# Loading V by head group in turn with the last quarters of w_out, in a fused attention and MLP kernel

## The chip, the cores and the metric

The kernel runs on one core of a Trainium2 chip. The metric is the device time of one execution in microseconds (us). The profile's own span is a little shorter than that time; both are given below.

## The reference

Attention over 8 batches, 12 heads, 448 tokens and a head dimension of 64, and then a two-layer MLP on its output (3584 tokens, model width 768, inner width 2048):

```python
scores = scale * np.matmul(q, k.transpose(0, 1, 3, 2))
scores = scores - np.max(scores, axis=-1, keepdims=True)
attn = np.exp(scores)
attn = attn / (np.sum(attn, axis=-1, keepdims=True) + 1e-09)
attn_out = np.matmul(attn, v)
...
x = attn_out.transpose(0, 2, 1, 3).reshape(B * S, H * D)
h = x @ w_in
g = h * (1.0 / (1.0 + np.exp(-h)))
return g @ w_out
```

All inputs and the output are float32 in memory; the kernel converts them to float16 as it loads them.

## The kernel before, in words

The twelve heads of a batch are taken in three head groups of four. A unit is one head group of one batch; the first batch is cut into five smaller units (`BEGIN`), so that work can start before all of it is there. For each unit the kernel loads K and Q (`load_k` into `rk`, `load_q` into `rq`), transposes them on VectorE (`turn_k` into `KT`, `turn_q`), multiplies them on TensorE into `s` (`scores`), takes the exponential on ScalarE into `E`, sums it over keys (`attend_sums`, the `a` that reads `T` and `half`, or for the first units the `a` that reads `ones`), and multiplies it with V (`attend`, the `a` that reads `V`). VectorE normalises the result into `xT`.

A batch that is through attention goes through the MLP: `ffn1` makes `h` from `w_in_t` and `xT`, ScalarE takes a tanh, VectorE's `gate` makes `G`, and products with `w_out_t` follow. The first two token tiles (`plain`, tiles `o`) use `w_out_t` as it is, in pieces of four of its sixteen row blocks, so a piece needs one quarter of `w_out`. The later ones (`product`, tiles `p`) work on pairs of token tiles with sums and differences of weights and gates, which takes fewer products; the sums of `w_out` (`combine_w`, tiles `D`) need all four quarters. The last two batches do the same with `w_in` (tiles `f`).

A product can stand on the whole array or in strips of 32 columns (`strips` in `times`): the strips are four matmuls for one, which run side by side, and are chosen where the work before was in strips as well (the mode "cols"). Scores are in the mode "rows". While TensorE has nothing else to do in the first stretch, it multiplies zeros (`run_zeros`, tile `z`, line 1602).

The order of all instructions is worked out ahead, in Python, while the kernel is built. `Order` holds a clock, a queue for each engine and estimated durations; at each step the loop at the end of the kernel takes the next work whose inputs are ready by these estimates, and the instructions are then written out in that order, each engine's for itself. On the chip each engine goes through its list in order and waits where a tile isn't there.

The loads are not reordered by it. POOL issues them in the order in which the `plan_` calls stand: `plan_k`, `plan_q`, `plan_v`, `plan_w_in` and `plan_w_out` append to `od.pool`. Their landing times are estimated in `Order.step`: a load takes slot after slot of one transfer queue (`dma_free`), starts at the earliest `DMA_START` after its issue, and is there `DMA_TAIL` after its transfer. At most `LOADS` = 8 of them may be under way, and in the built kernel each load waits for the eighth before it to land. K, Q and V also wait for a free buffer (three for `rk`, four for `rq`, two batches of V).

A V load is four transfers of 32 partitions each (`load_v`). The first batch's V is loaded for all twelve heads at once; from the second batch on it is loaded by head group. `w_out` comes in quarters of 768 KB (as float16).

Two estimates steer TensorE's order beside these: `LATE` shifts the time at which a V product of the first batch counts as ready against the landing of its V, and a weight's products count as ready once all loads in `ld_win` or `ld_wout` that they need have landed.

Of the kernel before, what the change touches and what calls it, by code (L numbers as in the profile page):

```python
# [18 lines left out]
PE_OUT = 0.20  # L19
HOP = 0.10  # L20
OVERLAP = {"ACT": 0.09, "DVE": 0.07}
LOADS, DMA_SLOW = 8, 1.45
DMA_ROW = 0.006
DMA_RATE = 13570.0
DMA_START = 1.2
DMA_TAIL = 1.5


def mm(n):
# [7 lines left out]
def rank(op):  # L37
    return (op.bias > -9) + (op.bias > 35)
# [65 lines left out]
class Order:  # L104
# [21 lines left out]
    def start(self, op):  # L126
        self.emit(op.emit)
        self.free[op.eng] = self.now + op.busy - OVERLAP.get(op.eng, 0.0)
        self.busy[op.eng] += op.busy
# [23 lines left out]
    def step(self):  # L153

        soon = []
        for eng in ("ACT", "DVE"):
            if self.free[eng] > self.now:
                soon.append(self.free[eng])
                continue
            best, urgent = None, None  # L160
            for op in self.wait[eng]:
                at = op.ready()
                if at is None:
                    continue
                if at > self.now:
                    soon.append(at)
                    if op.bias <= -10 and (urgent is None or at < urgent):
                        urgent = at
                elif best is None or (rank(op), at + op.bias) < best[0]:
                    best = ((rank(op), at + op.bias), op)  # L170
            if best and best[1].bias >= 0 and eng == "DVE" and urgent is not None:
                if urgent < self.now + self.shy * best[1].busy:
                    continue
            if best:
                self.wait[eng].remove(best[1])
                self.start(best[1])
                soon.append(self.free[eng])
        if self.free["POOL"] > self.now:
            soon.append(self.free["POOL"])
        elif self.pool:  # L180
            op, took, ring, gate = self.pool[0]
            at = 0.0
            if ring is not None:
                at = ring.when(1)
            if at is not None and len(self.sent) >= LOADS:
                at = max(at, self.sent[-LOADS].done + HOP)
            if at is not None and gate is not None:
                g = gate()
                at = None if g is None else max(at, g)
            if at is not None and at <= self.now:  # L190
                self.pool.pop(0)
                if ring is not None:
                    ring.take()
                self.start(op)
                self.sent.append(op)
                took += DMA_SLOW if len(self.sent) == 3 else 0.0
                self.dma_free = max(self.dma_free, self.now + DMA_START) + took
                op.done = self.dma_free + DMA_TAIL
                soon.append(self.free["POOL"])
            elif at is not None:  # L200
                soon.append(at)
        return soon
# [3 lines left out]
def kernel(  # L206
# [13 lines left out]
    DFF = moe_w_in.shape[1]  # L220
    HG = 4
    NG = NH // HG
# [8 lines left out]
    NFF = DFF // 128  # L231
# [6 lines left out]
    NPL = 4  # L238
    EAGER = 1
    HALVES = 0  # L240
    NEAR, LATE = 0.15, -0.9
    COLD, FIRST = 8.5, 47
    SHY = 0.5
    AWAIT = 0.0
# [5 lines left out]
    NB0 = len(BEGIN)  # L250
# [52 lines left out]
    def load_q(n):  # L303
        b, hg, g0, g1 = units[n]
        t = sb.tile([128, (g1 - g0) * D], FP16, name=f"rq_{n}", tag="rq", bufs=NRQ)
        nc.gpsimd.dma_start(out=t, in_=group_of(q, b, hg)[:, D * g0 : D * g1])  # L306
        rawq[n] = t

    def form(b, hg):
        n = NG * b + hg  # L310
        if n in LONES:
            return "lone"
        return ("low", "high")[(n - sum(x < n for x in LONES)) % 2]


    def load_v(b, hg0, hg1, x):
        if b not in VT:
            VT[b] = sb.tile([128, NH, NCH, D], FP16, name=f"V_{b}", tag="V", bufs=2)
        hs = slice(HG * hg0, HG * hg1)
        kind = form(b, hg0)  # L320
        if x == 0 and kind != "lone":
            lo = 64 if kind == "low" else 0
            nc.gpsimd.memset(VT[b][lo : lo + 64, hs, NCH - 1, :], 0.0)
        first, count = X_TOK[kind][x]
        nc.gpsimd.dma_start(  # L325
            out=VT[b][32 * x : 32 * (x + 1), hs, 0:count, :],
            in_=v[b, hs].rearrange("h (i g) d -> i h g d", g=TPP)[
                :, :, first : first + count, :
            ],
        )  # L330


    def load_w_in(c, f0, f1):
        nc.gpsimd.dma_start(
            out=w_in_t[:, 2 * c : 2 * c + 2, f0:f1],
            in_=moe_w_in[256 * c : 256 * (c + 1), f0:f1].rearrange(
                "(p j) f -> p j f", j=2
            ),
        )

    def load_w_out(f0, f1):
        nc.gpsimd.dma_start(
            out=w_out_t[:, f0:f1],
            in_=moe_w_out[128 * f0 : 128 * f1].rearrange("(f p) m -> p f m", p=128),
        )
# [106 lines left out]
    def add_e(n, step):  # L452
        if step == 0:
            T[n] = sb.tile([128, HG, S], FP16, name=f"T_{n}", tag="T", bufs=NT_)
        nc.vector.tensor_tensor(  # L455
            out=T[n],
            in0=T[n] if step else E[(n, 0)],
            in1=E[(n, step + 1)],
            op=ALU.add,
        )  # L460
# [55 lines left out]
    def inverse(ns, step, i=0):  # L516
        g0, g1 = units[ns[0]][2:]
        shape = [128, g1 - g0, 32]
        if step == 0:
            sT_t[ns[0]] = sb.tile(shape, FP32, name=f"sT_{ns[0]}", tag="sT", bufs=1)  # L520
            nc.vector.transpose(
                out=sT_t[ns[0]],
                in_=acc[(ns[0], 0)][:, 0 : 32 * (g1 - g0)].rearrange("p (g i) -> p g i", i=32),
            )
        elif step == 1:
            inv_t[ns[0]] = sb.tile(
                shape[:2] + [len(ns)], FP32, name=f"inv_{ns[0]}", tag="inv", bufs=2
            )
            nc.vector.reciprocal(
                out=inv_t[ns[0]], in_=sT_t[ns[0]][:, :, 0 : 32 : 32 // len(ns)]  # L530
            )
        else:
            n = ns[i]
            rdn_t[n] = sb.tile(shape, FP32, name=f"rdn_{n}", tag="rdn", bufs=2)
            nc.vector.transpose(
                out=rdn_t[n], in_=inv_t[ns[0]][:, :, i : i + 1].to_broadcast(shape)
            )
# [353 lines left out]
    def plan_k(b, hg):  # L891
        ld_k[(b, hg)] = od.load(128, 2 * D * TPP, lambda: load_k(b, hg), rk_ring)

    def plan_q(n):
        g0, g1 = units[n][2:]
        ld_q[n] = od.load(128, 2 * D * (g1 - g0), lambda: load_q(n), rq_ring)

    def plan_v(b, hg0, hg1):
        made = []
        for x in range(4):  # L900
            ring = v_ring if (x == 0 and hg0 == 0) else None
            heads, toks = HG * (hg1 - hg0), X_TOK[form(b, hg0)][x][1]
            made.append(
                od.load(32 * heads, 2 * D * toks, lambda x=x: load_v(b, hg0, hg1, x), ring)
            )
        for hg in range(hg0, hg1):
            ld_v[(b, hg)] = made

    def plan_w_in(f0, f1):
        made = [  # L910
            od.load(256, 2 * (f1 - f0), lambda c=c: load_w_in(c, f0, f1))
            for c in range(NG)
        ]
        for f in range(f0 // 128, f1 // 128):
            ld_win[f] = made

    def plan_w_out(f0, f1):
        wout_rows.append(f0)
        ld_wout.append(od.load(128 * (f1 - f0), 2 * DM, lambda: load_w_out(f0, f1)))
# [7 lines left out]
    plan_v(0, 0, NG)  # L927
    plan_q(3)
    plan_q(4)
    plan_w_in(0, DFF // 4)  # L930
    plan_w_in(DFF // 4, DFF // 2)
    plan_k(1, 0)
    plan_q(NB0)
    plan_w_in(DFF // 2, DFF)
    plan_k(1, 1)
    plan_q(NB0 + 1)
    plan_w_out(0, NFF // 4)
    plan_w_out(NFF // 4, NFF // 2)
    plan_k(1, 2)
    plan_q(NB0 + 2)  # L940
    for hg in range(NG):
        plan_v(1, hg, hg + 1)
    plan_w_out(NFF // 2, 3 * NFF // 4)
    plan_w_out(3 * NFF // 4, NFF)
    for n in range(NB0 + NG, NU):
        b, hg = units[n][:2]
        plan_k(b, hg)
# [750 lines left out]
```

## Time and profile before

| | |
|---|---|
| Median of 3 runs | 390.31 us (390.11 to 392.94) |
| The profiled execution | 390.07 us, span 388.3 us |
| TensorE (PE) | 380.2 us busy |
| VectorE (DVE) | 270.0 us |
| ScalarE (ACT) | 250.2 us |
| GpSimd (POOL) | 90.8 us, mostly issuing loads |

In the rows of the profile, PE is TensorE's matmuls, PEld its weight loads, and L577 is line 577 of the kernel before. A row of the order of time has the start in us, the duration in us, engine, line and operation, what is written and read, shapes and type, and the number of instructions that are merged. A bracket at its end is the time for which the engine stood idle before it, and what ended that. A row of waits has the engine and line, what it waited for, the total in us, how often, and the longest. "DMA to landing" is the time from a load's issue to the landing of its last byte, as the least, the median and the greatest of the group. GB/s counts bytes written. A row of the stages has the stretch in us, then for PE, PEld, DVE, ACT and POOL the busy time and the number of instructions, the granted TensorE clock, the share of the DMA engines and GB/s.

### The profile page before, as it was taken

How to read it: one execution, taken by the hardware profiler on the slowest of the kernel's cores; microseconds unless marked ns; L12 is line 12 of the kernel's file. 1: busy time of each engine (PE TensorE's matmuls, PEld its weight loads, DVE VectorE, ACT ScalarE, POOL GpSimd, SP SyncE). 2: the span in 40 equal slices, each digit the busy share in tenths (PEclk: the TensorE clock that was granted, in tenths of full speed). 3: DMA queues.
4: the chain of work that ended last, by engine and by line, in shares of the span. 5: the costliest groups of instructions: out<-in, count | busy, mean ns of one | idle time of the engine just before them, and what ended most of it. 6: DMA issues, size and time to landing. Idle time of an engine off the chain costs nothing.

```text
span 388.3 us, 10882 instructions
## 1 busy us (share of the span) xinstructions
PE 380.2 (98%) x4504; PEld 199.4 (51%) x4504; DVE 270.0 (70%) x544; ACT 250.2 (64%) x383; POOL 90.8 (23%) x175
## 2 busy tenths in 40 slices
PE   7999989999999999999999999999999999999995
PEld 3467755444554444455445554554445655556663
DVE  2565757989977696967798758567869964447441
ACT  4898864697775979676874667466783238882220
POOL 6742365507006331600643024000000000000000
PEclk9999999999999999999999999999999999999999
DMA  7999999908236763924956139002000130001333
GB/s 111 200 210 209 169 157 216 195 12 111 52 78 102 139 81 40 137 72 92 136 80 84 42 76 161 11 2 61 24 1 2 43 97 26 0 2 40 92 95 101
DMA packets 36002, 34.54 MB, mean 89 GB/s; under 512 B 11376, under 2 KB 35184, under 8 KB 35952
## 3 DMA queue, kind: packets, MB, share of 16 engines
q0 software_dynamic: 25456, 22.82, 39.9%
q1 hardware_dynamic: 10080, 10.53, 10.0%
q8 instruction: 35, 0.57, 0.7%
q10 hardware_dynamic: 416, 0.49, 0.4%
q14 instruction: 15, 0.12, 0.1%
HBM read 45.61 MB, written 11.01 MB: 146 GB/s over the span
## 4 chain that ended last, share of the span: by engine, by line
PE 88%; DMA 8%; POOL 1%; DVE 1%; issue 0%; ACT 0%; DVEq 0%; POOLq 0%
PE p L577 31%; PE h L577 24%; PE s L407 10%; PE a L470 9%; PE f L577 8%; DMA rq<-in_q_dram 6%; PE o L577 2%; DMA w_out_t<-in_moe_w_out_dram 2%; PE a L486 2%; PE z L1602 1%; PE z L470 1%; POOL V L325 1%; PE z L577 0%; DVE rq L378 0%; POOL rk L300 0%
## 5 line engine op out<-in xcount | busy, mean ns | idle before, releaser
L444 ACT ACTIVATE E<-s 128x896 f16<-128x896 f32 (+1 forms) x172 | 148.0, 916 | 32.3 <-PE s L407 31.7
L577 PE MATMUL h<-xT,w_in_t 128*32 128x448 f16 (+2 forms) x1308 | 116.0, 340 | 0.0
L577 PEld LDWEIGHTS <-w_in_t 128*32 128x32 f16 (+1 forms) x1392 | 71.7, 97 | 56.2 <-issue 11.3
L609 ACT ACTIVATE th<-h 128x448 f16<-128x448 f32 x95 | 51.8, 546 | 35.2 <-PE h L577 31.6
L577 PEld LDWEIGHTS <-G 128*128 128x128 f16 (+1 forms) x652 | 43.5, 97 | 33.7 <-issue 5.5
L868 ACT COPY ost<-p 128x384 f32<-128x384 f32 x52 | 24.9, 480 | 53.2 <-PE p L577 50.2
L653 DVE SCALAR_TENSOR_TENSOR G<-th,h 128x448 f16<-128x448 f16 (+1 forms) x80 | 44.0, 557 | 14.9 <-ACT th L609 14.5
L325 POOL DMA_DIRECT2D V<-in_v_dram x88 | 48.3, 560 | 16.5 <-DMA w_out_t<-in_moe_w_out_dram 6.1
L577 PE MATMUL p<-w_out_t,G 128*128 128x384 f16 (+1 forms) x376 | 49.6, 326 | 0.0
L407 PE MATMUL s<-rq,KT 32*128 32x448 f16 (+4 forms) x736 | 45.4, 345 | 1.5 <-DVE rq L378 1.4
L577 PEld LDWEIGHTS <-S 128*128 128x128 f16 (+1 forms) x408 | 29.9, 98 | 23.0 <-issue 3.1
L470 PE MATMUL a<-E,V 128*32 128x448 f16 (+3 forms) x800 | 40.3, 342 | 0.0
L306 POOL DMA_DIRECT2D rq<-in_q_dram x26 | 14.5, 559 | 100.0 <-PE s L407 90.5
L577 PE MATMUL p<-D,S 128*128 128x384 f16 (+1 forms) x256 | 37.2, 326 | 0.0
L874 DVE TENSOR_TENSOR ost<-p,ost 128x384 f32<-128x384 f32 x39 | 21.5, 550 | 14.1 <-PE p L577 11.2
L455 DVE TENSOR_TENSOR T<-E,E 128x1792 f16<-128x1792 f16 x20 | 21.7, 1083 | 11.9 <-ACT E L444 11.9
L470 PEld LDWEIGHTS <-V 128*32 128x32 f16 (+1 forms) x832 | 20.2, 96 | 18.5 <-issue 6.4
L565 DVE SCALAR_TENSOR_TENSOR xT<-a,rdn 128x448 f16<-128x448 f32 x44 | 26.4, 615 | 3.1 <-PE a L470 1.7
L407 PEld LDWEIGHTS <-KT 32*128 32x128 f16 (+2 forms) x832 | 13.5, 98 | 29.2 <-issue 27.0
L455 DVE TENSOR_TENSOR T<-T,E 128x1792 f16<-128x1792 f16 x20 | 21.7, 1084 | 9.3 <-ACT E L444 9.3
L360 DVE STREAM_TRANSPOSE KT<-rk 128x256 f32<-128x256 f32 (+3 forms) x48 | 16.5, 382 | 10.7 <-DMA rk<-in_k_dram 10.6
L577 PE MATMUL p<-w_out_t,S 128*128 128x384 f16 (+1 forms) x152 | 19.1, 326 | 0.0
(76 smaller groups left out, 334.1 us busy)
## 6 DMA issues: line engine op xcount, KB each, us to landing
out_dram<-ost SPq DMA_DIRECT2D x194, 48.0 KB, 1.7
rk<-in_k_dram POOLq DMA_DIRECT2D x24, 224.0 KB, 5.2
rq<-in_q_dram POOLq DMA_DIRECT2D x22, 224.0 KB, 5.6
w_out_t<-in_moe_w_out_dram POOLq DMA_DIRECT2D x4, 768.0 KB, 13.4
V<-in_v_dram POOLq DMA_DIRECT2D x43, 64.0 KB, 4.2
V<-in_v_dram POOLq DMA_DIRECT2D x40, 48.0 KB, 4.5
w_in_t<-in_moe_w_in_dram POOLq DMA_DIRECT2D x6, 256.0 KB, 7.5
w_in_t<-in_moe_w_in_dram POOLq DMA_DIRECT2D x3, 512.0 KB, 12.5
```

Source lines behind the costliest of these rows:

```text
L325: nc.gpsimd.dma_start(out=VT[b][32 * x : 32 * (x + 1), hs, 0:count, :], in_=v[b, hs].rearrange("h (i g) d -> i h g d", g=TPP)[:, :, first ...
L360: nc.vector.transpose(out=pairs[:, x:y, 0:count], in_=t[:, first : first + count * (y - x)].rearrange("p (x c) i -> p x c i", c=count),)
L407: nc.tensor.matmul(out=pS[p0 : p0 + 32 * (x1 - x0), h % 2, at : at + nq], lhsT=KT[(b, hg)][32 * h : 32 * (h + 1), c, x0:x1, :, e], rhs=QT[ ...
L444: nc.scalar.activation(out=E[(n, w)][0:kr, 2 * y : 2 * y + 2, 0:nk], in_=pS_t[(n, w, y)][0:kr, :, 0:nk], func=AF.Exp, scale=attn_scale,)
L455: nc.vector.tensor_tensor(out=T[n], in0=T[n] if step else E[(n, 0)], in1=E[(n, step + 1)], op=ALU.add,)
L470: nc.tensor.matmul(out=a[32 * h : 32 * (h + 1), 0:nq], lhsT=w, rhs=e[k0:k1, h, at : at + nq], start=start, stop=stop,)
L565: nc.vector.scalar_tensor_tensor(out=x3(b, cc)[:, cc % 3, 32 * g0 : 32 * g1], in0=acc[(n, part)][:, 0:nq], scalar=0.5, in1=rdn_t[n].rearra ...
L577: nc.tensor.matmul(out=out[i : i + cut], lhsT=w[:, i : i + cut], rhs=x, start=start, stop=stop, skip_group_check=True,)
L609: nc.scalar.activation(out=th, in_=h_t[(b, f, t0)][:, 0:n], func=AF.Tanh)
L653: nc.vector.scalar_tensor_tensor(out=dst[:, f, at + lo : at + hi], in0=th_t[(b, f, t0)][:, lo - t0 : hi - t0], scalar=1.0, in1=h_t[(b, f, ...
L868: nc.scalar.copy(out=ost(qd, *OUT[m]), in_=bank(qd, BANK[m]))
L874: nc.vector.tensor_tensor(out=t, in0=bank(qd, BANK[m]), in1=t, op=ALU.add)
```

## The change

The loads of the second batch's V, one head group at a time, alternate with the last two quarters of `w_out`; both quarters came behind all three groups. The other lines of the list of loads say the same in other words (`NB0` is 5, `DFF` 2048, `NFF` 16). The estimates by which the order is drawn change: from the seventh load on, a load starts `DMA_LATE` later and is there `DMA_MORE` later; `DMA_TAIL` is 1.3 in place of 1.5; `LATE` is -0.3 in place of -0.9.

```diff
+DMA_LATE, DMA_MORE = 1.0, 0.6
 LOADS, DMA_SLOW = 8, 1.45
 ...
-DMA_TAIL = 1.5
+DMA_TAIL = 1.3
 ...
-                self.dma_free = max(self.dma_free, self.now + DMA_START) + took
-                op.done = self.dma_free + DMA_TAIL
+                few = len(self.sent) < 7
+                start = self.now + DMA_START + (0.0 if few else DMA_LATE)
+                self.dma_free = max(self.dma_free, start) + took
+                op.done = self.dma_free + DMA_TAIL + (0.0 if few else DMA_MORE)
 ...
-    NEAR, LATE = 0.15, -0.9
+    NEAR, LATE = 0.15, -0.3
 ...
     plan_k(1, 2)
-    plan_q(NB0 + 2)
-    for hg in range(NG):
-        plan_v(1, hg, hg + 1)
-    plan_w_out(NFF // 2, 3 * NFF // 4)
-    plan_w_out(3 * NFF // 4, NFF)
+    plan_q(7)
+    plan_v(1, 0, 1)
+    plan_w_out(8, 12)
+    plan_v(1, 1, 2)
+    plan_w_out(12, 16)
+    plan_v(1, 2, 3)
     for n in range(NB0 + NG, NU):
```

More of the change, by code (lines that the diff above doesn't have):

```diff
@@ L929 @@
     plan_q(4)
-    plan_w_in(0, DFF // 4)
-    plan_w_in(DFF // 4, DFF // 2)
+    plan_w_in(0, 512)
+    plan_w_in(512, 1024)
     plan_k(1, 0)
-    plan_q(NB0)
-    plan_w_in(DFF // 2, DFF)
+    plan_q(5)
+    plan_w_in(1024, 2048)
     plan_k(1, 1)
-    plan_q(NB0 + 1)
-    plan_w_out(0, NFF // 4)
-    plan_w_out(NFF // 4, NFF // 2)
+    plan_q(6)
+    plan_w_out(0, 4)
+    plan_w_out(4, 8)
     plan_k(1, 2)
-    plan_q(NB0 + 2)
-    for hg in range(NG):
-        plan_v(1, hg, hg + 1)
-    plan_w_out(NFF // 2, 3 * NFF // 4)
-    plan_w_out(3 * NFF // 4, NFF)
+    plan_q(7)
[4 more added lines that the diff above has]
+    plan_v(1, 2, 3)
     for n in range(NB0 + NG, NU):
```

## The prediction

> **What bounds the kernel now.** I read the page first, then the waits of TensorE over the whole span, then TensorE's order of time around the one long wait, and last the queue of loads that this wait hangs on.
>
> ```profile
> span 388.3 us, 10882 instructions
> PE 380.2 (98%) x4504; PEld 199.4 (51%) x4504; DVE 270.0 (70%) x544; ACT 250.2 (64%) x383; POOL 90.8 (23%) x175
> ...
> PE o L577 <- DMA w_out_t<-in_moe_w_out_dram: 1.7, 1, 1.7
> PE s L407 <- DVE rq L378: 1.4, 2, 1.0
> PE z L1602 <- DVE zeros L273: 1.0, 1, 1.0
> ```
>
> TensorE works for 380.2 of 388.3 us. Its list of waits has three rows in all, and two of them belong to the first 10 us, where the first tiles arrive. So in the body of the kernel one wait is left to win: 1.7 us for a quarter of `w_out`. Everything else could only be won by giving TensorE less work, which a changed order of loads does not do. This is the place:
>
> ```profile
> 53.67 0.57 PE L407 MATMUL s<-rq,KT 32*128 32x448 f16 x8
> 54.18 1.47 PE L577 MATMUL o<-w_out_t,G 128*128 128x384 f16 x8
> 57.34 0.81 PE L577 MATMUL o<-w_out_t,G 128*128 128x384 f16 x4 [1.69 <-DMA w_out_t<-in_moe_w_out_dram]
> 58.08 0.58 PE L407 MATMUL s<-rq,KT 32*128 32x448 f16 x8
> 58.59 2.12 PE L577 MATMUL o<-w_out_t,G 128*128 128x384 f16 x12
> 60.65 0.60 PE L407 MATMUL s<-rq,KT 32*64 32x448 f16 x16
> 61.18 2.12 PE L577 MATMUL o<-w_out_t,G 128*128 128x384 f16 x12
> 63.24 0.56 PE L486 MATMUL a<-T,half 128*32 128x448 f16 x8
> ```
>
> The eight products from 54.18 use the first two quarters of `w_out`; the four from 57.34 are the first that read the third quarter, and they stand idle until it lands. The queue that issued it, on POOL, with the loads around it (a row's bracket names the load whose landing freed the issue; every load waits for the eighth before it):
>
> ```profile
> 36.80 0.55 POOL L325 DMA_DIRECT2D V<-in_v_dram  x1 [0.19 <-issue]
> ...
> 40.54 0.54 POOL L325 DMA_DIRECT2D V<-in_v_dram  x1 [2.86 <-DMA w_out_t<-in_moe_w_out_dram]
> 44.29 0.54 POOL L325 DMA_DIRECT2D V<-in_v_dram  x1 [3.20 <-DMA w_out_t<-in_moe_w_out_dram]
> 45.42 0.54 POOL L325 DMA_DIRECT2D V<-in_v_dram  x1 [0.59 <-DMA rk<-in_k_dram]
> 46.50 0.54 POOL L325 DMA_DIRECT2D V<-in_v_dram  x1 [0.54 <-DMA rq<-in_q_dram]
> 47.08 0.30 POOL L323 MEMSET V<- 64x256 f16 x1
> 47.34 2.15 POOL L325 DMA_DIRECT2D V<-in_v_dram  x4
> 49.47 1.51 POOL L342 DMA_DIRECT2D w_out_t<-in_moe_w_out_dram  x2
> 50.95 0.58 POOL L300 DMA_DIRECT2D rk<-in_k_dram  x1
> 51.48 0.59 POOL L306 DMA_DIRECT2D rq<-in_q_dram  x1
> ```
>
> The last two quarters are issued at 49.47, behind eight small V loads whose issue slots came free only one by one. What the 16 engines moved between 40 and 60 us, in half-microsecond slices, shows what that costs:
>
> ```profile
> GB/s 206 215 215 202 208 217 205 223 182 183 171 172 118 85 69 37 78 71 86 98 95 113 45 52 143 169 203 197 212 212 209 203 212 212 209 215 209 212 205 214
> ```
>
> From 46 to 52 us the rate falls from about 208 to a mean of 79 GB/s: the only loads that had slots were small, and the big ones had not been issued. That is 6 x (1 - 79/208) = 3.7 us of transfer time lost, just ahead of the quarter that TensorE waits for.
>
> **The change, part by part.** First the order of loads. In the changed program POOL issues the second batch's V of head group 0 (four loads), the third quarter of `w_out`, V of group 1, the fourth quarter, V of group 2. No load is added, removed or resized. The times of landing by issue, for four groups (the V loads of 31.65 to 36.80, those of 47.34, the two quarters of 49.47, and rq of 51.48):
>
> ```profile
> DMA to landing us min/median/max: 10.7/12.0/14.9
> ...
> DMA to landing us min/median/max: 2.2/2.3/2.5
> ...
> DMA to landing us min/median/max: 7.8/9.3/10.8
> ...
> DMA to landing us min/median/max: 12.0/12.0/12.0
> ```
>
> The third quarter takes the slot that today's first V of group 1 has, 40.54. V of group 0 lands from 31.65 + 14.9 = 46.6 to 36.80 + 10.7 = 47.5, four loads 0.3 us apart; the queue lands in order. A quarter behind other traffic takes 3.75 us (the first two freed their slots at 40.54 and 44.29). So the third quarter lands near 47.5 + 3.75 = 51.2, in place of 49.47 + 7.8 = 57.3, and TensorE asks for it at 54.18 + 8 x 0.163 = 55.5: 4.3 us of room, and the 1.69 us wait is gone.
>
> V of group 1 follows at slots 44.29, 45.42, 46.50 and about 47.1 and lands by 51.2 + 4 x 0.3 = 52.4. The fourth quarter's slot is freed by a V of group 0 near 47.0, so it is issued about 47.6; alone it could not land before 47.6 + 7.8 = 55.4, and in the queue it lands at 52.4 + 3.75 = 56.2. The changed order of TensorE wants it sooner than today's: twelve products, one stretch of scores of 0.51 us, then the products of the fourth quarter at once, so at 54.18 + 12 x 0.163 + 0.51 = 56.6. The room is 0.4 us, less whatever TensorE is earlier by then. I take a new wait of 0.1 us; bounds follow under the rivals.
>
> Behind it V of group 2 lands near 57.5, then rk and rq of the third batch near 58.6 and 59.8, instead of 51.48 + 12.0 = 63.5 for that rq. V of groups 1 and 2 lands up to 6 us later than now and costs nothing: its first reader stands after the sums of 63.24.
>
> Second, the refitted load times. They do not change an instruction's cost; they move TensorE's, ScalarE's and VectorE's orders. Before 50 us little moves: the program has 111 blocks of 128 zero columns in place of 114, and one block of the second token piece's products is drawn ahead of those that need the last part of `w_in`.
>
> ```profile
> 16.60 0.23 PE L1602 MATMUL z<-zeros 128*128 128x128 f16 x1
> ...
> 47.87 1.70 PE L470 MATMUL a<-E,V 128*32 128x448 f16 x32
> ...
>   DMA w_in_t<-in_moe_w_in_dram: 0.3, 1
> ```
>
> Three zero blocks less are at most 3 x 0.23 = 0.7 us, but most of them only fill time in which a transposed tile is awaited; the wait for `w_in` in the weight loads is 0.3 us. Together I take 0.3. It cannot be more than 0.4: the V products at 47.87 need the last V of group 0, which lands at 47.5 in either order, so a TensorE that is earlier still waits there.
>
> From 60 us on TensorE's order differs widely, and from what stands at 205 us in this trace it is the same again. The scores of the third batch come ahead of three pieces of work that came first so far:
>
> ```profile
> 63.81 1.47 PE L577 MATMUL o<-w_out_t,G 128*32 128x384 f16 x32
> 65.11 3.20 PE L470 MATMUL a<-E,V 128*32 128x448 f16 x64
> 68.14 2.12 PE L577 MATMUL o<-w_out_t,G 128*32 128x384 f16 x48
> ```
>
> That is about 6.5 us of lead, which the scores of the following batches keep, while products of `w_in` and `w_out` change places between them. Some stretches change from whole-array to 32-column form (1518 weight loads of `w_in_t` for 1392, fewer of `G`). Two rows of the chain give the price for the same two blocks of h:
>
> ```profile
> 73.82 2.38 PE h L577 x12
> ...
> 91.83 2.27 PE h L577 x48
> ```
>
> 2.27 in narrow form against 2.38 (with its entry from the scores): nothing to lose. The switches between the forms are as many within a handful (159 for 158 between scores and the rest), so I take 0 here, with 0.2 either way.
>
> Third, what may now come late. The first scores of the third batch stood behind 70 us; they follow now after the fourth quarter's products: 56.6 + 16 x 0.163 + 0.53 + 12 x 0.163 + 0.68 = 62.4. They need rq at 59.8 and its transposition.
>
> ```profile
> 68.91 0.63 DVE L378 STREAM_TRANSPOSE rq<-rq 128x448 f32<-128x448 f32 x1
> ```
>
> 59.8 + 0.63 = 60.4, 2 us ahead. If the queue did not speed up, rq at 63.5 would make them wait 63.5 + 0.63 - 62.4 = 1.7 us, all of the gain. I count 0.
>
> **Sum**, against the profiled execution's 390.07 us (span 388.3 and 1.8 around it): -1.69 for the third quarter, -0.3 for the early part, +0.1 for the fourth quarter = -1.9, so 388.2. The median of the runs shown is 390.31, 0.24 above the profiled one; I stay with 388.2.
>
> The Trainium skill, "DMA: Bandwidth & Descriptors", section "Anatomy of one DMA", gives a load issued here about 2.0 us plus its bytes at 436 GB/s. For a quarter's 768 KB that is an estimate of 3.8 us, so by that section the quarter issued at 49.47 would land at 53.3 and there would be no wait to remove; the sum would then be -0.2 alone. The trace has 7.8 for it, and the row at 57.34 shows the wait, so the measurement decides.
>
> **The rivals.**
>
> *The fourth quarter takes the third's place.* If V of group 1 costs 0.54 us for each load instead of 0.3 (the four of 47.34 are issued 2.15 / 4 = 0.54 apart and land within 2.5 us of their issue, so that is what they take when nothing is queued behind), the fourth quarter lands at 51.2 + 2.2 + 3.75 = 57.1, a wait of 0.5, or with the early gain of 0.3 one of 0.8: 388.6 to 388.9. A transfer that is later by another 0.5 us, from V of group 0 on, makes it 389.4. For it speaks how small the room is; against it the 0.3 us that V of group 0 shows behind other traffic.
> The Trainium skill, "DMA: Bandwidth & Descriptors", section "Bandwidth", has 0.95 us for a load of 64 KB; by that estimate V of group 1 takes 3.8 us, the fourth quarter lands at 58.8 and the sum would be 390.3. Neither the 0.3 nor the 0.54 of the trace agrees with it.
>
> *The hole only moves: no change.* If the engines find nothing to do elsewhere instead (POOL still gives out V of group 1 one slot at a time, ahead of the fourth quarter), the block of loads ends when it ends now, rq lands at 63.5, and the first scores of the third batch wait the 1.7 us worked out above: 389.9. Against it: the third quarter alone gives the engines 3.75 us of work for exactly that time.
>
> *A quarter behind V loads starts late: slower.* Today's third quarter landed 5.9 us after the V before it (the last of the four is issued at 47.34 + 3 x 0.54 = 48.9 and lands by 51.4; then 57.3), not 3.75. If that is what a big load costs behind small ones, both quarters now pay it: 47.5 + 5.9 = 53.4, V of group 1 at 54.6, the fourth at 60.5. TensorE would wait there 60.5 - 56.6 = 3.9 us, against 2.0 won: 392.0. It decides against the change from a landing of 58.6 on. Against it: 5.9 is explained by the issue at 49.47 and by the hole in GB/s.
>
> *The middle eats the gain.* Scores that come 6 to 7 us earlier ask ScalarE and VectorE for their work in another mixture, and in 70 to 100 us VectorE is close to full:
>
> ```profile
> 90.00:100.00 10.00, 10.00 (x196) 4.72 (x198) 9.80 (x24) 7.49 (x12) 5.73 (x12) 1.00 0.97 137
> ```
>
> A wait of a VectorE instruction or two (0.6 to 1.1 us) would leave 388.8 to 389.3. Against it: TensorE is never idle there today.
>
> *The refit gives more.* If the early zeros are on the path after all and the fourth quarter is on time: 387.5.
>
> **How the numbers follow.** Forecast 0.6 (387.7 to 388.7); fourth quarter or middle eats a part 0.21 (388.7 to 389.4); the hole moves 0.07 (389.9); slower 0.06 (392.0); more 0.06 (387.5). The likeliest is 388.2. The range from 387.4 to 390.2 leaves out the slower case and the outer edges of the rest. About what a measurement of this kernel can tell from no change is 1%, 3.9 us: no term here reaches that in favour, so faster by over 1% has 0.04; slower by over 1% needs the late quarter and a second wait, 0.05; 0.91 lies within.
>
> **What would show it.** Right: TensorE's waits have no row for `w_out` over 0.3 us; GB/s holds near 200 through 46 to 52 us; the third quarter is issued near 40.5 and the first scores of the third batch start near 62. Wrong: a wait for `w_out` ahead of the fourth quarter's products, an rq that lands after 61.7, or a new TensorE wait for VectorE or ScalarE between 60 and 130 us.

## The result, and the profile after

The changed kernel takes 388.15 us (median of 11 runs, 387.33 to 389.12), the kernel before 390.35 us beside it: a ratio of 0.9933, 95% interval 0.9909 to 0.9957. The forecast was 388.2. The profiled execution is at 388.23 us with a span of 386.4, against 390.07 and 388.3 before.

The page of the profile and the waits of TensorE:

```profile
span 386.4 us, 10919 instructions
PE 379.9 (98%) x4522; PEld 199.4 (52%) x4522; DVE 270.2 (70%) x544; ACT 250.2 (65%) x383; POOL 90.7 (23%) x175
...
PE s L410 <- DVE rq L381: 1.5, 1, 1.5
PE z L1606 <- DVE zeros L276: 1.0, 1, 1.0
```

TensorE's work is the same to 0.3 us, and the row for `w_out` is gone from its waits. What is left there belongs to the first 11 us. TensorE's order of time at the place where the wait was:

```profile
53.65 0.57 PE L410 MATMUL s<-rq,KT 32*128 32x448 f16 x8
54.16 2.12 PE L580 MATMUL o<-w_out_t,G 128*128 128x384 f16 x12
56.21 0.57 PE L410 MATMUL s<-rq,KT 32*128 32x448 f16 x8
56.72 2.77 PE L580 MATMUL o<-w_out_t,G 128*128 128x384 f16 x16
59.42 0.60 PE L410 MATMUL s<-rq,KT 32*64 32x448 f16 x16
59.96 2.12 PE L580 MATMUL o<-w_out_t,G 128*128 128x384 f16 x12
...
62.70 0.57 PE L410 MATMUL s<-rq,KT 32*128 32x448 f16 x8
```

Twelve products stand in one piece where there were eight, a hole, and four. The sixteen from 56.72 begin with the four that read the fourth quarter. The first product with `w_out` starts at 54.16 in place of 54.18, so nothing was won ahead of it; the scores of the third batch begin at 62.70 in place of 70.20. POOL's loads, then the landing of the two quarters issued at 40.72 and 47.74 and of the rq issued at 53.27, and GB/s from 40 to 60 us in half-microsecond slices:

```profile
40.72 0.75 POOL L345 DMA_DIRECT2D w_out_t<-in_moe_w_out_dram  x1 [3.19 <-DMA w_out_t<-in_moe_w_out_dram]
...
47.74 0.75 POOL L345 DMA_DIRECT2D w_out_t<-in_moe_w_out_dram  x1
...
53.27 0.57 POOL L309 DMA_DIRECT2D rq<-in_q_dram  x1
```

```profile
DMA to landing us min/median/max: 10.7/10.7/10.7
...
DMA to landing us min/median/max: 8.6/8.6/8.6
...
DMA to landing us min/median/max: 6.7/6.7/6.7
...
GB/s 206 212 210 201 227 199 211 218 189 180 197 215 199 204 220 215 203 203 195 189 179 193 190 212 213 212 200 247 171 177 184 177 203 218 194 189 176 147 143 167
```

The third quarter lands at 40.72 + 10.7 = 51.4, the fourth at 47.74 + 8.6 = 56.3, the rq at 53.27 + 6.7 = 60.0. The hole in the transfers between 46 and 52 us is full. The fourth quarter is there 0.3 to 0.4 us before TensorE reads it at 56.72.

### The profile page after: what moved, and what is told of

The parts are those of the page before. It is cut to its first block, busy times and chain, and to the rows that moved or that the text cites. A ratio compares the mean times of both kernels' runs of the same rounds, so it can differ in the third digit from the quotient of the medians.

```text
span 386.4 us, 10919 instructions
## 1 busy us (share of the span) xinstructions
PE 379.9 (98%) x4522; PEld 199.4 (52%) x4522; DVE 270.2 (70%) x544; ACT 250.2 (65%) x383; POOL 90.7 (23%) x175
## 4 chain that ended last, share of the span: by engine, by line
PE 96%; DMA 2%; POOL 0%; issue 0%; DVE 0%; ACT 0%; POOLq 0%
PE p L580 31%; PE h L580 29%; PE s L410 11%; PE a L473 11%; PE f L580 8%; PE o L580 3%; PE a L489 2%; DMA rq<-in_q_dram 2%; PE z L1606 1%; PE z L473 0%; PE z L580 0%; POOL rk L303 0%; DVE rq L381 0%; POOL rq L309 0%; ACT ost L871 0%
## 5 line engine op out<-in xcount | busy, mean ns | idle before, releaser
L580 PEld LDWEIGHTS <-w_in_t 128*32 128x32 f16 (+1 forms) x1518 | 72.8, 97 | 54.5 <-issue 9.7
L612 ACT ACTIVATE th<-h 128x448 f16<-128x448 f32 x95 | 51.7, 545 | 37.7 <-PE h L580 34.1
```

What stands on the lines that cost most here:

```text
L580: nc.tensor.matmul(out=out[i : i + cut], lhsT=w[:, i : i + cut], rhs=x, start=start, stop=stop, skip_group_check=True,)
L612: nc.scalar.activation(out=th, in_=h_t[(b, f, t0)][:, 0:n], func=AF.Tanh)
```

## The experiments

The theory: TensorE lost 1.85 us from start to start (57.34 - 54.18, less eight products of 0.163 each) because one quarter of `w_out` was not there when TensorE's list came to it, and any change that ends this ends all of it. The main rival: the newly drawn order of the engines carries the gain. All kernels below compute the whole reference. In the first group POOL's order is exchanged as the drawn list is written out, so that loads and engine orders come apart:

```diff
-    for _, _, fn in sorted(od.out, key=lambda x: x[:2]):
-        fn()
 ...
+    mine = [op.emit for op in v0 + v1 + v2 + w3 + w4]
+    todo = [op.emit for op in v0 + w3 + v1 + w4 + v2]
 ...
+    for fn in drawn:
+        (todo.pop(0) if fn in mine else fn)()
```

Here `v0` to `v2` are the second batch's V by head group, `w3` and `w4` the quarters, and `drawn` is the sorted list. Each ratio is against the kernel before, timed in the same group; the experiments fall into three groups, whose medians of the kernel before are 390.15, 390.88 and 389.91 us.

**The new order of loads under the old orders of the engines** (the diff above on the kernel before).

> The kernel before with its orders of TensorE, ScalarE and VectorE as they are; only POOL issues the ten loads in the new order (V group 0, third quarter of w_out, V group 1, fourth quarter, V group 2). Theory 1 (the gain is the earlier slot of the third quarter): it lands near 51.3 us, the wait of 1.7 us at 55.5 is gone, the fourth quarter lands near 56.4 and is asked for at 60.5 - 1.85 = 58.7, so no new wait: 1.85 us less, a ratio of 0.9953. Theory 2 (the gain is the newly drawn order of the engines, for which the list of loads is only one cause): no gain without it, a ratio of 1.000, the third quarter early and TensorE late elsewhere.

388.43 us, ratio 0.9954 (0.9936 to 0.9972). The gain is there without one instruction of TensorE, ScalarE or VectorE in another place. TensorE's waits no longer name `w_out`. The third quarter lands at 40.60 + 10.7 = 51.3, and its first reader comes at 54.69 + 8 x 0.163 = 56.0:

```profile
PE s L407 <- DVE rq L378: 1.9, 2, 1.4
PE z L1602 <- DVE zeros L273: 1.0, 1, 1.0
PE a L470 <- DVE xT L554: 0.3, 1, 0.3
...
54.69 2.12 PE L577 MATMUL o<-w_out_t,G 128*128 128x384 f16 x12
...
40.60 0.75 POOL L342 DMA_DIRECT2D w_out_t<-in_moe_w_out_dram  x1 [3.20 <-DMA w_out_t<-in_moe_w_out_dram]
...
DMA to landing us min/median/max: 10.7/10.7/10.7
```

**The new orders of the engines under the old order of loads** (the same edit on the changed kernel, with `todo` in the order v0, v1, v2, w3, w4).

> The changed kernel with the orders of TensorE, ScalarE and VectorE as they are; only POOL issues the ten loads in the old order (three groups of V, then both quarters). Theory 1: the wait of 1.85 us is back, and because this order asks for the fourth quarter 0.65 + 0.55 us after the third one's landing at 57.3, and it lands at 61.0, TensorE waits there 2.5 us more; the early shifts are worth 0: slower than before by 2.5 us, a ratio of 1.006. Theory 2: the drawn order carries the gain, 388.2, a ratio of 0.9945.

394.30 us, ratio 1.0105 (1.0082 to 1.0129): slower, as the theory said, and by more than it said.

```profile
53.65 1.47 PE L580 MATMUL o<-w_out_t,G 128*128 128x384 f16 x8
56.37 0.81 PE L580 MATMUL o<-w_out_t,G 128*128 128x384 f16 x4 [1.25 <-DMA w_out_t<-in_moe_w_out_dram]
57.11 0.58 PE L410 MATMUL s<-rq,KT 32*128 32x448 f16 x8
60.10 4.35 PE L580 MATMUL o<-w_out_t,G 128*128 128x384 f16 x16 [2.41 <-DMA w_out_t<-in_moe_w_out_dram]
```

Both waits came where they were expected, the first one shorter (1.25 us for 1.85). But the sixteen products from 60.10 take 4.35 us; in the changed kernel they take 2.77. The stages show why (column PEclk, after the POOL column):

```profile
56.00:58.00 2.00, 1.32 (x12) 0.50 (x12) 2.00 (x3) 0.28 (x1) 0.56 (x1) 1.00 1.16 210
58.00:60.00 2.00, 0.00 (x0) 0.00 (x0) 0.34 (x1) 0.63 (x1) 0.00 (x0) 1.00 1.16 210
60.00:62.00 2.00, 1.90 (x10) 1.01 (x10) 0.70 (x2) 1.05 (x2) 1.35 (x3) 0.77 1.27 197
62.00:64.00 2.00, 2.00 (x8) 0.91 (x6) 1.72 (x3) 0.24 (x1) 1.47 (x4) 0.50 1.22 207
64.00:66.00 2.00, 2.00 (x25) 0.86 (x24) 1.63 (x2) 0.93 (x2) 1.32 (x4) 0.87 1.30 235
```

After the second wait the granted clock falls to 0.77, 0.50 and 0.87 for some six microseconds, which accounts for the 1.6 us. This profiled execution, at 393.21 us, is the fastest of the five; the two slowest, at 394.53 and 394.93, have a mean granted clock of 0.991 where it has 0.996, and no profile shows where they lost it.

**The new list of loads with the old estimates**, all orders drawn anew (the kernel before with the last hunk of the change alone).

> The new list of loads with the old estimates (DMA_START, DMA_TAIL and LATE as before, no DMA_LATE or DMA_MORE), all orders drawn anew from that. Theory 1: the third quarter lands near 51.3 and is asked for near 55.5, the fourth lands near 56.4 and is asked for near 56.6: at most 0.3 us of a wait, a ratio of 0.9950 to 0.996. Theory 2 (the refit carries the gain): 1.000.

388.44 us, ratio 0.9957 (0.9943 to 0.9972). The refit is not needed for the gain: TensorE's waits name no `w_out`, and the twelve products stand in one piece.

```profile
PE s L407 <- DVE rq L378: 1.6, 2, 1.3
PE z L1603 <- DVE zeros L273: 1.0, 1, 1.0
...
54.20 2.12 PE L577 MATMUL o<-w_out_t,G 128*128 128x384 f16 x12
```

**The refit with the old list of loads**, all orders drawn anew (the changed kernel with the three groups of V ahead of both quarters).

> The old list of loads with the new estimates, all orders drawn anew. In the drawn order TensorE now takes products of the first two quarters for the second token tile ahead of those that need the third quarter. Theory 1 in its strict form (only an earlier landing helps): the quarter still lands at 57.3 and the 1.85 us stay, a ratio of 1.000. Theory 2 (a drawn order that knows the landing time fills the wait with other work): TensorE asks for the third quarter only after about 12 products, a stretch of scores and more products, near 57, and waits 0.3 us at most: a ratio of 0.9950 to 0.996.

387.91 us, ratio 0.9945 (0.9925 to 0.9966). Nor is the list. The rival holds here: the third quarter is still late, issued at 49.03 and there 7.6 us later, at 56.6, which is 0.7 us before its landing in the kernel before and 5.2 us behind that in the changed kernel, and the transfers have their hole as before:

```profile
54.09 2.12 PE L580 MATMUL o<-w_out_t,G 128*128 128x384 f16 x12
56.14 0.57 PE L410 MATMUL s<-rq,KT 32*128 32x448 f16 x8
56.65 2.12 PE L580 MATMUL o<-w_out_t,G 128*128 128x384 f16 x12
...
49.03 1.50 POOL L345 DMA_DIRECT2D w_out_t<-in_moe_w_out_dram  x2
...
DMA to landing us min/median/max: 7.6/9.1/10.6
...
GB/s 209 209 215 204 214 209 203 221 186 176 170 158 116 99 47 85 61 92 72 128 105 64 37 104 197 215 236 178 203 212 206 200 212 218 209 206 212 217 207 205
```

The drawing that knows the landing time puts four products of the second token tile, which need the first quarter only, where TensorE's idle time would be, and four more that need the second quarter ahead of the first reader of the third, which comes at 56.65 + 4 x 0.163 = 57.3. TensorE does not wait for `w_out` at all. So the hole in the transfers costs nothing by itself, and the two halves of the change are two ways to the same 1.85 us; together they give it once.

**The third quarter alone moved ahead** (old engine orders, `todo` in the order v0, w3, v1, v2, w4).

> The kernel before with its orders as they are; only the third quarter of w_out is issued ahead of V group 1, the fourth stays behind all of V. Theory 1 (each quarter must have landed when it is asked for; a quarter's landing is 7.8 us after its issue at the least): the third quarter costs nothing; the fourth waits for the slot of the first V of group 1 (lands near 51.8), is issued near 52.3, lands near 60.1 and is asked for at 59.3: a new wait of 0.8 us, 1.05 us less than before in all, a ratio of 0.997. Rival (the third quarter alone matters): 1.85 us less, 0.9953.

388.29 us, beside a kernel before of 390.88 in that group, ratio 0.9914 (0.9887 to 0.9941). The ratio looks better than the others because six of the 17 executions of the kernel before in that group have a mean granted clock of 0.994 or 0.995 and take 391.8 to 393.4 us; the median of its other eleven is 390.43. The 0.8 us that I expected did not come; the rival was right:

```profile
54.20 2.12 PE L577 MATMUL o<-w_out_t,G 128*128 128x384 f16 x12
...
59.35 2.12 PE L577 MATMUL o<-w_out_t,G 128*128 128x384 f16 x12
...
L342 POOL DMA_DIRECT2D w_out_t<-in_moe_w_out_dram x1: 757/757/757, 51.7 to 51.7; - x1
...
DMA to landing us min/median/max: 7.0/7.0/7.0
```

I had taken 7.8 us as the least time from a quarter's issue to its landing. Here it took 7.0, from 51.7 to 58.7, and the first reader comes at 59.35. The issue was also 0.6 us earlier than the 52.3 that I had taken.

**The fourth quarter last of all** (the changed kernel, `todo` in the order v0, w3, v1, v2, w4).

> The changed kernel with its orders as they are; only the fourth quarter is issued last, behind V group 2. It lands near 60.2 and this order asks for it at 56.7: one idle stretch of 3.5 us. Theory A (an idle stretch costs its own length): 388.1 + 3.5 = 391.6, a ratio of 1.003. Theory B (a stretch of this length also lowers the granted clock, as the kernel with the new order and the old loads had it with 0.77, 0.50 and 0.87 in 60 to 66 us, some 1.5 us of work more): 393.1, a ratio of 1.007, with a granted clock near 0.5 for about 3 us behind the stretch.

392.53 us, ratio 1.0023 (0.9997 to 1.0048), with runs from 390.3 to 393.5. The profiled execution, at 393.22, goes by theory B:

```profile
56.30 0.57 PE L410 MATMUL s<-rq,KT 32*128 32x448 f16 x8
60.01 4.44 PE L580 MATMUL o<-w_out_t,G 128*128 128x384 f16 x16 [3.13 <-DMA w_out_t<-in_moe_w_out_dram]
...
60.00:62.00 2.00, 1.99 (x9) 1.03 (x9) 0.70 (x2) 1.14 (x2) 1.41 (x3) 0.72 1.25 194
62.00:64.00 2.00, 2.00 (x8) 0.91 (x6) 1.81 (x3) 0.15 (x1) 1.49 (x3) 0.50 1.26 205
64.00:66.00 2.00, 2.00 (x25) 0.86 (x24) 1.54 (x2) 0.98 (x2) 1.31 (x4) 0.93 1.25 228
```

3.1 us of idleness and then sixteen products in 4.44 us for 2.77. Not every execution pays all of it. By the mean granted clock of each execution there are two kinds: eight have 0.991 to 0.996 and take 391.8 to 393.5 us, 392.8 in the mean; the other four have 0.999 or 1.000 and take 390.3 to 391.5, 390.8 in the mean. So both theories happen, and the fall of the clock goes with some 2.0 us. That the four lie 0.8 us below theory A's 391.6 is not explained; only a profile of one of them could show its wait.

**Both quarters ahead of V groups 1 and 2** (the changed kernel, `todo` in the order v0, w3, w4, v1, v2).

> The changed kernel with its orders as they are; POOL issues both quarters directly behind V group 0, then V groups 1 and 2. The fourth quarter then waits for the slot of the second quarter (free at 44.2), lands near 55.2 in place of 56.4, and has 1.5 us of room in place of 0.3; V of group 1 lands near 56.5, long before 64. Theory 1 (a quarter that is there in time gives nothing more): the time of the changed kernel, 0.9945. Rival (the narrow room still costs something in some executions): 0.1 to 0.5 us less than the changed kernel, 0.993 to 0.9943.

388.54 us, ratio 0.9916 (0.9886 to 0.9946) beside the same 390.88. The median is not below the changed kernel's; more room for the fourth quarter gives nothing that was seen. In its profile the third quarter lands at 52.1 and the fourth at 56.0, 1.3 us before it is read.

**LATE at -0.9 in the changed kernel**, all orders drawn anew, in two groups; the second time beside the changed kernel itself.

> The changed kernel with LATE at -0.9 again, all orders drawn anew: 117 blocks of zeros for 111, and from the trace of before and after TensorE reaches the first product with w_out at the same time. Theory 1 (the zeros fill time in which TensorE waits for ScalarE's exponentials or a landing, so their number costs nothing): the time of the changed kernel, a ratio of 0.9945. Rival (the forecast's term of 0.3 us for the early part): 0.3 to 0.6 us more than the changed kernel, 0.9955 to 0.996.

> The changed kernel once more, beside the one with LATE at -0.9 on the same chip, since the two were not timed together so far. Theory 1 (the early part is worth nothing): the two medians within 0.15 us. Rival (the early part is worth the forecast's 0.3 us): this one 0.3 to 0.5 us below the other.

> The changed kernel with LATE at -0.9, once more, beside the changed kernel. Theory 1: the same median within 0.15 us. Rival: 0.3 to 0.5 us above.

First 388.93 us, ratio 0.9928 (0.9901 to 0.9955), 0.39 above the kernel of the experiment before, which has the changed kernel's engine orders, on the same chip. Then 388.82, ratio 0.9977 (0.9965 to 0.9988), against 388.29 for the changed kernel, ratio 0.9955 (0.9935 to 0.9975): 0.53 more. The rival is favoured twice, but the intervals against the kernel before overlap, so it is not shown beyond doubt. Nor is it the forecast's term: that was for 111 blocks of zeros in place of the 114 of the kernel before, and this kernel has 117. For 111 beside 114 the groups disagree: in one the refit alone (111) takes 387.91 us and the two kernels with 114 take 388.43 and 388.44; in the other the third quarter alone (114) takes 388.29 and both quarters first (111) 388.54.

**One table over all.** Span, start of the first product with `w_out`, and what lies between it and the end, from the profiled executions:

| Kernel | span | first `w_out` product | from there to the end |
|---|---|---|---|
| before | 388.3 | 54.18 | 334.1 |
| changed | 386.4 | 54.16 | 332.2 |
| loads only | 386.9 | 54.69 | 332.2 |
| list, old estimates | 386.5 | 54.20 | 332.3 |
| refit alone | 386.3 | 54.09 | 332.2 |
| third quarter only | 386.5 | 54.20 | 332.3 |
| both quarters first | 387.0 | 54.68 | 332.3 |
| changed, again | 386.6 | 54.27 | 332.3 |
| LATE back (first group) | 387.1 | 54.79 | 332.3 |
| LATE back (second group) | 387.8 | 55.51 | 332.3 |
| order only | 391.4 | 53.65 | 337.8 |
| fourth last | 391.4 | 54.25 | 337.2 |

The nine executions of seven kernels in which TensorE has no wait for `w_out` agree to 0.1 us behind that product, though their middle parts stand in two quite different orders. That is TensorE's work from there on without a wait, and the kernel before was 1.9 above it. What differs between them lies before that product, and there the same engine orders gave 53.65 to 54.68. No version here beats the changed kernel clearly, and none of the nine shows a wait of TensorE behind that product that would point to one that does.

## Why the prediction was right

*The wait.* The term was 1.69 us, and the place and the cause were right: the kernel with the new loads alone shows it. Its size is 1.85 from start to start, since the profile's idle time counts from the modelled end of a matmul, 0.16 later than the next would have started.

*The landings.* Third quarter 51.2 forecast and 51.4 measured, fourth 56.2 and 56.3, the rq 59.8 and 60.0, first scores of the third batch 62.4 and 62.7. One queue in order, 3.75 us for a quarter and 0.3 for a V, with the eighth load before it as the gate, was enough here. The step that read 7.8 us as a least time for a lone quarter was too strict: 7.0 to 7.6 occurred.

*The fourth quarter.* I took 0.1 us for a wait; there was none. The rival that it takes the third's place was real in kind: the same order with a later fourth quarter gave 392.53.

*The early part.* The term of -0.3 does not show in the profiled executions (54.16 against 54.18), where the same engine orders differ by up to a microsecond. The comparisons with LATE give 0.39 and 0.53 us for six blocks of zeros, not for these three, and kernels with 111 and 114 blocks differ by 0.5 us one way in one group and 0.25 the other way in another. What the term is worth stays open.

*The sum.* In the profiled executions the wait gave 1.85 us, and the other two terms nothing that shows: 390.07 to 388.23, a change of 1.84 for a forecast of 1.89. The wait was taken 0.16 too small, and the -0.3 and the +0.1 made up for that, so part of the close agreement is luck. The medians fell by 2.2 us, as the median of the kernel before is 0.28 above its profiled execution; in the groups of experiments its median is raised by executions with a lower granted clock.

*The middle.* Zero was right: 332.2 to 332.3 with either order.

*The rivals.* A late start of a big load behind V loads fell: the third quarter landed 3.7 us behind the V before it (36.98 + 10.7 = 47.7 to 51.4). A wait in the middle fell as well, by the last column of the table. The slower case existed, but elsewhere: engine orders drawn for one list of loads and run with another. And what I named as the cause of the loss, the hole in the transfers, was only one side of it. The refit alone leaves the hole and takes the whole gain, 387.91 us. So one step failed beside the right time: "Everything else could only be won by giving TensorE less work, which a changed order of loads does not do" looks for the gain in the loads alone, and the refit was counted as worth nothing at the wait itself.

The Trainium skill, "DMA: Bandwidth & Descriptors", section "Anatomy of one DMA", would have a lone quarter landed after an estimated 3.8 us, counted by the 768 KB that are written. The runs show 7.0 to 7.8 for a quarter issued when only small V loads were under way, so they disagree by about a factor of two.

## What to carry to other kernels

A wait of a saturated engine on a load can be taken away from either side, by an earlier slot in the queue or by an order that asks later; here the two gains did not add, and a gap in the transfer rate is not a loss unless an engine waits behind it. An order that is fixed ahead belongs to the landing times for which it was drawn: with another list of loads the same order was 4 us slower than the kernel before. An idle stretch of the matrix engine can cost more than its length: behind 2.4 to 3.1 us of it the clock was lower in most executions here, and that has to be in the price, as a chance.

## What the runs showed of the hardware that was not expected

In the profiled execution of the kernel before, a wait of 1.69 us left the granted TensorE clock at 1.00:

```profile
56.00:58.00 2.00, 0.66 (x4) 0.29 (x3) 1.09 (x1) 0.00 (x1) 0.14 (x1) 1.00 1.17 212
58.00:60.00 2.00, 2.00 (x18) 1.02 (x18) 0.00 (x0) 1.31 (x2) 0.41 (x1) 1.00 1.16 210
```

Two waits of 1.25 and 2.41 us within five microseconds, and a single one of 3.13 us, were each followed by a clock of 0.72 to 0.77, 0.50 and 0.87 to 0.93 in three stages of 2 us, and by 16 products in 4.4 us for 2.8. My price for the slower rival, 3.9 us of pure wait, lacked this.

The lower clock did not come in every execution, and it came more often where there was more idle time. A mean granted clock of 0.996 or less stands in all 5 executions of the kernel whose profile has the waits of 1.25 and 2.41 us, in 8 of 12 of the one with 3.13, in 9 of 59 of the kernel before in the three groups of experiments, and in 2 of 80 of the kernels in whose profiles TensorE does not wait for `w_out`. The nine of the kernel before take 392.5 us in the mean, the other fifty 390.1. There is no profile of one of the nine, so it is not shown that their clock fell behind the wait for the third quarter.

The Trainium skill, "TensorE: Matmul & The Clock Gate", section "What's actually happening", has the clock halved after one idle window of about 3.4 us and full again after a busy one of that length. The 0.50 agrees; the fall came here after less idle time than that, a single idle stretch of 3.13 us, and after 2.41 with 1.25 shortly before it.

Loads of 48 and 64 KB queued behind a quarter landed about 0.3 us apart (V of group 1 in the changed kernel, at 51.8, 52.1, 52.4 and 52.7), while the same kind issued into an almost empty queue took 2.2 to 2.5 us from issue to landing (the four of 47.34 in the kernel before).
